# Dense layer, Mish, dense layer on one core: the first block of tokens in 128-token tiles, part of it transposed by DMA

## The chip, the core and the metric

The kernel runs on one core of a Trainium2 chip. The core has five engines with instruction streams of their own: TensorE (PE in the profile; PEld are its weight loads), VectorE (DVE), ScalarE (ACT), GpSimd (POOL) and SyncE (SP), which here only issues transfers. Transfers issued by SP and by ACT run on 16 DMA engines. The metric is device time in microseconds (us), the median of several runs.

## The reference

```python
h = jnp.einsum("bsd,df->bsf", x, w1) + b1
sp = jnp.log1p(jnp.exp(-jnp.abs(h))) + jnp.where(h > 0, h, jnp.zeros_like(h))
act = h * jnp.tanh(sp)
return jnp.einsum("bsf,fd->bsd", act, w2)
```

x is (1, 2048, 512), w1 (512, 1792), b1 (1792), w2 (1792, 512), all bf16. So there are 2048 tokens; h is x w1 + b1, act is Mish of h, and the output is act w2.

## The kernel before, in words

**Tiling.** Tokens go in four blocks of 512 (`NSB`), each of four tiles of 128. The first product wants x with its 512 features on the partitions, so x must be transposed: xT has four slices k of 128 features (`KT` = 4). The 1792 hidden features are 14 tiles f (`FT`). One tile of the first product, `mm1(t)`, is four matmuls (k = 0 to 3) of 128 rows by 512 tokens into one PSUM bank; ScalarE then computes Mish with b1 as bias from that bank into a_sb (`mish`, L167). One tile of the second product, `mm2(i)`, is 14 matmuls (one for each f) of 128 tokens by 512 outputs into a bank; VectorE casts it to bf16 (L202) and SP stores it (L180). The last tile, and only that one, is done in two parts so that its first part can be cast and stored while the second is computed.

**Order.** TensorE's order is written out by hand (L207 to L224): the first block's special start, then `mm1` for f = 4 to 13, then for each block its four `mm2` and the next block's 14 `mm1`. PSUM has eight banks. Tile t of the first product uses bank 4 + t mod 4 (`bank1`, L161), so a tile waits for the Mish of the tile four before it; the second product uses banks 0 to 3.

**Waits.** A `Stream` is one engine's queue. `mark` makes an instruction count up the engine's semaphore and returns a token, `wait` makes a queue wait for a token, `load` issues a transfer and returns its token. An engine's waits and instructions are executed in the order of the program; what stands behind a wait on its queue waits too. This is so for SP and ACT when they issue transfers.

**Loads (L88 to L102).** SP issues, in this order: the two halves (256 tokens each) of the first block of x, untransposed, into x_nat; w1 for f = 4 to 7; w1 for f = 8 to 13; w2; and the other three blocks of x by transposing DMAs straight into xT. ACT issues w1 for f = 0 to 3, in two pieces of two k slices, and b1. No wait stands between these.

**The start of the first block.** TensorE first runs six matmuls on a constant tile (`dummy`, L117) whose results nobody reads. Then `half_T(0)` (L122) transposes tokens 0 to 255 on TensorE, eight transposes of 128x128 against the identity; the results go from PSUM to xT by VectorE for even k and ScalarE for odd k, 256 columns at a time. Two more dummies of 256 columns follow. `first_mm1(h, ks)` (L140) then runs the first product for f = 0 to 3 and one half of the tokens, 256 columns a matmul: half 0 with k = 0, 1; then `half_T(1)`; half 0 with k = 2, 3; the transpose of b1 (L213), which arrives as 14 rows and is wanted as 14 columns; then half 1 with all k. Both halves of a tile share a bank and each starts a group of its own (`start=(k == 0)`).

The first block's tokens are dealt to the partitions so that a partition holds two neighbouring tokens (`x0v`), and its outputs are stored through the same view (`o0v`).

The change and the prediction's steps touch the loads, `half_T`, `first_mm1`, the dummies, `bank1`, `mm2`'s last tile, and the order at the end.

Of the kernel before, what the change touches and what calls it, by code (L numbers as in the profile page):

```python
# [4 lines left out]

P = 128
N_WARM = 6
FILL = (256, 256)


class Stream:
# [20 lines left out]
def bass_standalone__dense_activation_mish__prompt_kernel(  # L32
# [8 lines left out]
    ACT = mybir.ActivationFunctionType  # L41
    ALU = mybir.AluOpType
    BF, F32 = dt.bfloat16, dt.float32

    _, S, D = x.shape
    F = w1.shape[1]
    KT, FT, SBW = D // P, F // P, 512
    NSB, JT, H = S // SBW, SBW // P, D // 2
    assert (S, D, F) == (2048, 512, 1792)
    x2, out2 = x[0], out[0]  # L50
    w1v = w1.rearrange("(k p) f -> p k f", p=P)
    w2v = w2.rearrange("(j p) d -> p j d", p=P)
    F0 = 4

    with ExitStack() as es:
        def sb(name, shape, t):
            return es.enter_context(nc.sbuf_tensor(name, shape, t))

        x_nat = sb("x_nat", [P, JT, D], BF)
        xT = sb("xT", [P, KT, S], BF)  # L60
        w1_sb = sb("w1_sb", [P, KT, F], BF)
        w2_sb = sb("w2_sb", [P, FT, D], BF)
        b1_nat = sb("b1_nat", [FT, P], BF)
        b1_sb = sb("b1_sb", [P, FT], F32)
        ones = sb("ones", [P, P], BF)
        ident = sb("ident", [P, P], BF)
        a_sb = sb("a_sb", [P, NSB * FT, SBW], BF)
        o_sb = sb("o_sb", [P, NSB * JT, D], BF)
        ps = es.enter_context(nc.psum_tensor("ps", [P, 8, 512], F32))

        def sem(name):
            return es.enter_context(nc.semaphore(name))

        sp = Stream(nc.sync, None)
        pe = Stream(nc.tensor, sem("c_pe"))
        dve = Stream(nc.vector, sem("c_dve"))
        act = Stream(nc.scalar, sem("c_act"))
        pool = Stream(nc.gpsimd, sem("c_pool"))

        def load(q, dst, src, name, transpose=False):  # L80
            s = sem(name)
            (q.eng.dma_start_transpose if transpose else q.eng.dma_start)(dst, src).then_inc(s, 16)
            return (s, 16)

        n_pre = len(nc.cur_bb.bb.instructions)


        x0v = x2[0:SBW, :].rearrange("(h p j) d -> p h j d", h=2, j=2)  # L88
        t_xn = [load(sp, x_nat[:, 2 * h:2 * h + 2, :], x0v[:, h], "s_xn%d" % h) for h in range(2)]
        t_w1k = []  # L90
        for k in (0, 2):
            t_w1k += [load(act, w1_sb[:, k:k + 2, 0:F0 * P], w1v[:, k:k + 2, 0:F0 * P], "s_w1k%d" % k)] * 2
        t_b1 = load(act, b1_nat[:, :], b1.rearrange("(j p) -> j p", p=P), "s_b1")
        t_w1 = {}
        for a, b in ((4, 8), (8, FT)):
            t = load(sp, w1_sb[:, :, a * P:b * P], w1v[:, :, a * P:b * P], "s_w1_%d" % a)
            for f in range(a, b):
                t_w1[f] = t
        t_w2 = load(sp, w2_sb[:, :, :], w2v, "s_w2")
        t_xT = [None]  # L100
        for s in range(1, NSB):
            t_xT.append(load(sp, xT[:, :, s * SBW:(s + 1) * SBW], x2[s * SBW:(s + 1) * SBW, :], "s_xT%d" % s, True))  # L102

# [3 lines left out]
        t_id = pool.mark(pool.eng.affine_select(ident[:, :], ones[:, :], pattern=[[1, P]], compare_op=ALU.is_equal,  # L107
                                                fill=0.0, base=0, channel_multiplier=-1))
        act.eng.preload_act_table(ACT.Mish)  # L109


        warm = sb("warm", [P, 512], BF)
        pe.wait(dve.mark(nc.vector.memset(warm[:, :], 1.0)))  # L113
        c_w, c_m = warm[:, 0:P], warm

        def dummy(n=512):
            nc.tensor.matmul(ps[:, 7, 0:n], c_w, c_m[:, 0:n], start=True, stop=True)  # L117

        HB = SBW // 2
        t_cp = [[None] * KT for _ in range(2)]  # L120

        def half_T(h):  # L122

            pe.wait(t_xn[h])
            for k in range(KT):
                if h == 1:
                    pe.wait(t_cp[0][k])
                psb = ps[:, k, 0:HB // 2].bitcast(BF)
                for j in range(2):
                    mm = nc.tensor.transpose(psb[:, j * P:(j + 1) * P], x_nat[:, 2 * h + j, k * P:(k + 1) * P], ident[:, :])  # L130
                t = pe.mark(mm)
                dst = xT[:, k, h * HB:(h + 1) * HB]
                if k % 2 == 0:
                    dve.wait(t)
                    t_cp[h][k] = dve.mark(nc.vector.tensor_copy(dst, psb))  # L135
                else:
                    act.wait(t)
                    t_cp[h][k] = act.mark(act.eng.activation(dst, psb, ACT.Copy))  # L138

        def first_mm1(h, ks):  # L140

            cs = slice(h * HB, (h + 1) * HB)
            for k in ks:
                for f in range(F0):
                    pe.wait(t_w1k[k], t_cp[h][k])
                    mm = nc.tensor.matmul(ps[:, 4 + f, cs], w1_sb[:, k, f * P:(f + 1) * P], xT[:, k, cs],  # L146
                                          start=(k == 0), stop=(k == KT - 1))
                    if h == 1 and k == KT - 1:
                        mish(f, pe.mark(mm))

        for _ in range(N_WARM):
            dummy()
        pe.wait(t_id)
        half_T(0)
        for n in FILL:
            dummy(n)


        t_mish = {}

        def bank1(t):  # L161
            return 4 + t % 4

        def mish(t, t_mm):
            act.wait(t_b1c, t_mm)
            f = t % FT
            t_mish[t] = act.mark(act.eng.activation(a_sb[:, t, :], ps[:, bank1(t), :], ACT.Mish, bias=b1_sb[:, f:f + 1]))  # L167

        def mm1(t):
            s, f = divmod(t, FT)  # L170
            pe.wait(t_mish.get(t - 4), t_w1.get(f), t_xT[s])
            for k in range(KT):
                mm = nc.tensor.matmul(ps[:, bank1(t), :], w1_sb[:, k, f * P:(f + 1) * P],  # L173
                                      xT[:, k, s * SBW:(s + 1) * SBW], start=(k == 0), stop=(k == KT - 1))
            mish(t, pe.mark(mm))

        def store(q, i, lo, hi, tok):
            q.wait(tok)
            rows = out2[i * P:(i + 1) * P, :] if i >= JT else o0v[:, i // 2, i % 2, :]
            q.eng.dma_start(rows[:, lo:hi], o_sb[:, i, lo:hi]).then_inc(s_out, 16)  # L180

        s_out = sem("s_out")
        o0v = out2[0:SBW, :].rearrange("(h p j) d -> p h j d", h=2, j=2)
        n_out = 0
        t_ev = {}

        def mm2(i):
            nonlocal n_out
            s, j = divmod(i, JT)
            pe.wait(t_w2)  # L190
            last = i == NSB * JT - 1
            parts = [(0, H, i % 4), (H, D, (i + 1) % 4)] if last else [(0, D, i % 4)]
            for lo, hi, bank in parts:
                pe.wait(*([t_ev[bank]] if bank in t_ev else [t_b1c, t_cp[1][1], t_cp[1][3]]))
                for f in range(FT):
                    t = s * FT + f
                    pe.wait(t_mish[t])
                    mm = nc.tensor.matmul(ps[:, bank, 0:hi - lo], a_sb[:, t, j * P:(j + 1) * P], w2_sb[:, f, lo:hi],  # L198
                                          start=(f == 0), stop=(f == FT - 1))
                t_mm = pe.mark(mm)  # L200
                dve.wait(t_mm)
                t_ev[bank] = dve.mark(nc.vector.tensor_copy(o_sb[:, i, lo:hi], ps[:, bank, 0:hi - lo]))  # L202
                store(sp, i, lo, hi, t_ev[bank])
                n_out += 1


        first_mm1(0, (0, 1))  # L207
        half_T(1)
        first_mm1(0, (2, 3))
        pe.wait(t_b1)  # L210
        psb1 = ps[:, 0, 256:256 + FT // 2].bitcast(BF)
        pe.wait(t_cp[1][0])
        t_b1t = pe.mark(nc.tensor.transpose(psb1, b1_nat[:, :], ident[0:FT, 0:FT]))  # L213
        dve.wait(t_b1t)
        t_b1c = dve.mark(nc.vector.tensor_copy(b1_sb[:, :], psb1))  # L215
        first_mm1(1, range(KT))
        for t in range(F0, FT):
            mm1(t)
        for s in range(NSB):
            for j in range(JT):  # L220
                mm2(s * JT + j)
            if s + 1 < NSB:
                for f in range(FT):
                    mm1((s + 1) * FT + f)  # L224
# [37 lines left out]
```

## Time and profile before

| what | us |
|---|---|
| median of 11 runs | 106.59 |
| lowest and highest | 106.06, 107.3 |
| the profiled execution | 107.13 |
| its span, from first to last instruction | 105.9 |
| busy: TensorE, ScalarE, VectorE | 101.9, 40.6, 13.0 |
| last x half landed, after its issue | 4.1 |
| first, last L146 matmul start | 4.61, 9.57 |
| first L173 matmul starts | 10.59 |
| last CAST starts | 103.85 |

Busy times are sums over one execution's span; TensorE's include matmuls whose ends are modelled and overlap, so starts of matmuls are a better guide than their durations. The time around the span, 107.13 - 105.9 = 1.2 us, belongs to the execution and not to any engine. A line such as L146 is a line of the kernel as printed above. In the chain of work that ended last, each piece is what its successor waited for, or what stood before it on its engine.

### The profile page before, as it was taken

Reading aid. Unit: us, or ns where it says so; the run is one execution under the profiler, and the core shown is the slowest. Engines: PE = TensorE matmul, PEld = TensorE weight load, DVE = VectorE, ACT = ScalarE, POOL = GpSimd, SP = SyncE. Lnnn points to the kernel's source line nnn. Section 1 sums busy time; section 2 is a strip of 40 time slices with the busy share of each in tenths; the row PEclk is TensorE's granted clock in tenths of the full one; section 3 lists DMA queues with packets and bytes.
Section 4 is the critical chain, followed back from the end, with each engine's and each line's share of the span. In section 5 each row is a group of like instructions: output and inputs, shape, how many; then the busy total and the mean of one; then the engine's idle time right before and its main releaser. Section 6 shows DMA issues by size and latency. Waiting matters only on the chain.

```text
span 105.9 us, 1127 instructions
## 1 busy us (share of the span) xinstructions
PE 101.9 (96%) x494; PEld 49.5 (47%) x503; DVE 13.0 (12%) x23; ACT 40.6 (38%) x61; POOL 0.6 (1%) x6
## 2 busy tenths in 40 slices
PE   7997999999999999999999999999999999999992
PEld 2675444444444444444444444444444444444481
DVE  1210000022210000022112000021122000011241
ACT  3423988400007887500005888600005777700000
POOL 2000000000000000000000000000000000000000
DMA  5999999911111000001111000001111000001111
GB/s 138 372 373 352 346 246 219 99 42 48 50 50 50 0 0 6 0 0 50 50 50 50 0 0 3 0 6 50 50 50 50 0 0 0 0 0 56 50 50 50
DMA packets 12417, 7.94 MB, mean 75 GB/s; under 512 B 6652, under 2 KB 12156, under 8 KB 12412
## 3 DMA queue, kind: packets, MB, share of 16 engines
q1 hardware_dynamic: 11840, 7.34, 26.4%
q10 hardware_dynamic: 572, 0.53, 1.6%
q8 instruction: 4, 0.07, 0.3%
q14 instruction: 1, 0.01, 0.0%
HBM read 4.20 MB, written 2.10 MB: 59 GB/s over the span
## 4 chain that ended last, share of the span: by engine, by line
PE 96%; issue 1%; DVE 1%; ACT 1%; ACTq 0%
PE ps L198 46%; PE ps L173 42%; PE ps L146 4%; PE ps L117 3%; PE ps L130 1%; ACT a_sb L167 1%; DVE warm L113 0%; DVE o_sb L202 0%; PE ps L213 0%; ACTq L24 0%
## 5 line engine op out<-in xcount | busy, mean ns | idle before, releaser
L167 ACT ACTIVATE a_sb<-ps,b_sb 128x512 bf16<-128x512 f32 x56 | 37.9, 688 | 47.0 <-PE ps L173 44.9
L198 PE MATMUL ps<-w_sb,a_sb 128*128 128x512 bf16 (+1 forms) x234 | 48.8, 366 | 0.2
L173 PE MATMUL ps<-xT,w_sb 128*128 128x512 bf16 x203 | 45.1, 379 | 1.0 <-ACT a_sb L167 0.7
L198 PEld LDWEIGHTS ps<-w_sb,a_sb 128*128 128x128 bf16 x238 | 23.3, 98 | 25.3
L173 PEld LDWEIGHTS ps<-xT,w_sb 128*128 128x128 bf16 x208 | 20.3, 98 | 25.1 <-ACT a_sb L167 0.8
L202 DVE CAST o_sb<-ps 128x512 bf16<-128x512 f32 (+1 forms) x17 | 11.2, 660 | 84.8 <-PE ps L198 84.8
L146 PE MATMUL ps<-xT,w_sb 128*128 128x256 bf16 x32 | 4.9, 310 | 0.0
L117 PE MATMUL ps<-warm 128*128 128x512 bf16 (+1 forms) x8 | 3.4, 577 | 0.8 <-DVE warm L113 0.8
L146 PEld LDWEIGHTS ps<-xT,w_sb 128*128 128x128 bf16 x32 | 3.4, 111 | 0.7
L138 ACT ACTIVATE xT<-ps 128x256 bf16<-128x256 bf16 x4 | 1.4, 382 | 2.9 <-PE ps L130 2.9
L109 ACT ACT_TABLE_LOAD x1 | 1.3, 1283 | 1.8 <-issue 1.8
L130 PEld LDWEIGHTS ps<-ident,x_nat 128*128 128x128 bf16 x16 | 1.6, 130 | 0.7 <-issue 0.6
L117 PEld LDWEIGHTS ps<-warm 128*128 128x128 bf16 x8 | 1.0, 140 | 1.9 <-issue 1.1
L135 DVE COPY xT<-ps 128x256 bf16<-128x256 bf16 x4 | 1.1, 292 | 5.4 <-PE ps L130 5.3
L130 PE MATMUL ps<-ident,x_nat 128*128 128x128 bf16 x16 | 1.8, 274 | 0.0
L113 DVE MEMSET warm<- 128x512 bf16 x1 | 0.5, 485 | 0.2 <-issue 0.2
L107 POOL TENSOR_SCALAR_AFFINE_SELECT ident<-ones 128x128 bf16<-128x128 bf16 x1 | 0.3, 293 | 0.1
L215 DVE CAST b_sb<-ps 128x14 f32<-128x14 bf16 x1 | 0.2, 173 | 0.8 <-PE ps L213 0.8
L105 POOL MEMSET ones<- 128x128 bf16 x1 | 0.2, 204 | 0.0
L213 PEld LDWEIGHTS ps<-ident,b_nat 14*128 14x128 bf16 x1 | 0.1, 91 | 0.2 <-issue 0.2
L213 PE MATMUL ps<-ident,b_nat 14*128 14x14 bf16 x1 | 0.2, 178 | 0.0
L247 POOL MEMSET const-bfloat16-1.0<- 128x1 bf16 x1 | 0.1, 101 | 0.0
(3 smaller groups left out, 0.3 us busy)
## 6 DMA issues: line engine op xcount, KB each, us to landing
out_dram<-o_sb SPq DMA_DIRECT2D x15, 128.0 KB, 1.7
w_sb<-in_w_dram SPq DMA_DIRECT2D x1, 1792.0 KB, 12.1
w_sb<-in_w_dram SPq DMA_DIRECT2D x1, 768.0 KB, 7.5
x_nat<-in_x_dram SPq DMA_DIRECT2D x2, 256.0 KB, 3.5
w_sb<-in_w_dram ACTq DMA_DIRECT2D x2, 256.0 KB, 4.2
w_sb<-in_w_dram SPq DMA_DIRECT2D x1, 512.0 KB, 5.9
out_dram<-o_sb SPq DMA_DIRECT2D x2, 64.0 KB, 1.5
xT<-in_x_dram SPq DMA_TRANSPOSE x3, 6.1
```

Of the source, the lines that this page charges most:

```text
L109: act.eng.preload_act_table(ACT.Mish)
L113: pe.wait(dve.mark(nc.vector.memset(warm[:, :], 1.0)))
L117: nc.tensor.matmul(ps[:, 7, 0:n], c_w, c_m[:, 0:n], start=True, stop=True)
L130: mm = nc.tensor.transpose(psb[:, j * P:(j + 1) * P], x_nat[:, 2 * h + j, k * P:(k + 1) * P], ident[:, :])
L135: t_cp[h][k] = dve.mark(nc.vector.tensor_copy(dst, psb))
L138: t_cp[h][k] = act.mark(act.eng.activation(dst, psb, ACT.Copy))
L146: mm = nc.tensor.matmul(ps[:, 4 + f, cs], w1_sb[:, k, f * P:(f + 1) * P], xT[:, k, cs], start=(k == 0), stop=(k == KT - 1))
L167: t_mish[t] = act.mark(act.eng.activation(a_sb[:, t, :], ps[:, bank1(t), :], ACT.Mish, bias=b1_sb[:, f:f + 1]))
L173: mm = nc.tensor.matmul(ps[:, bank1(t), :], w1_sb[:, k, f * P:(f + 1) * P], xT[:, k, s * SBW:(s + 1) * SBW], start=(k == 0), stop=(k == KT ...
L198: mm = nc.tensor.matmul(ps[:, bank, 0:hi - lo], a_sb[:, t, j * P:(j + 1) * P], w2_sb[:, f, lo:hi], start=(f == 0), stop=(f == FT - 1))
L202: t_ev[bank] = dve.mark(nc.vector.tensor_copy(o_sb[:, i, lo:hi], ps[:, bank, 0:hi - lo]))
L213: t_b1t = pe.mark(nc.tensor.transpose(psb1, b1_nat[:, :], ident[0:FT, 0:FT]))
```

## The change

The first block goes by tiles of 128 tokens, and its second half comes transposed by DMA.

- Loads: SP issues x tile 0, x tile 1 (128 tokens each, plain rows, so `x0v` and `o0v` go), b1 (after VectorE has zeroed b1_nat, which is now 128x128), then waits for the last of w1's first pieces (`t_w1k[2]`), then issues the transposing DMA of tokens 256 to 511 into xT, w1 for f = 8 to 13, w2, and the other three transposing DMAs. ACT issues w1 for f = 0 to 3 in three pieces (k = 0, k = 1, k = 2 and 3) and w1 for f = 4 to 7 in two.
- The memset of the dummies' operand is 128 columns wide and stands first on VectorE; the dummies are 16 of 128 columns, and 2 after the first transposes.
- `part_T(j)` transposes one tile of 128 tokens, four transposes; all copies to xT are VectorE's.
- `first_mm1(js, fks)` runs any tiles js and pairs (f, k). The order: tile 0 with k = 0; transposes of tile 1; tile 0 with k = 1; tile 1 with k = 0, 1; both with k = 2; b1's transpose; both with k = 3; then f = 4 to 7 for both tiles, k outermost; then tiles 2 and 3 together for f = 0 to 7, f outermost.
- Banks: in the first block f = 4 to 7 use banks 0 to 3, all others stay at 4 + t mod 4. One table `t_bank` holds what each bank waits for. Each bank has one group: one start (tile 0, k = 0), one stop (tiles 2-3, k = 3).
- The last output tile is parted at column 384 instead of 256.

```diff
-N_WARM = 6
-FILL = (256, 256)
+N_WARM = 16
+N_FILL = 2
...
-        x_nat = sb("x_nat", [P, JT, D], BF)
+        x_nat = sb("x_nat", [P, 2, D], BF)
...
-        x0v = x2[0:SBW, :].rearrange("(h p j) d -> p h j d", h=2, j=2)
-        t_xn = [load(sp, x_nat[:, 2 * h:2 * h + 2, :], x0v[:, h], "s_xn%d" % h) for h in range(2)]
-        t_w1k = []
+        warm = sb("warm", [P, P], BF)
+        t_warm = dve.mark(nc.vector.memset(warm[:, :], 1.0))
+        t_b1z = dve.mark(nc.vector.memset(b1_nat[:, :], 0.0))
+        t_xa = load(sp, x_nat[:, 0, :], x2[0:P, :], "s_xa")
+        t_w1k = [load(act, w1_sb[:, k, 0:F0 * P], w1v[:, k, 0:F0 * P], "s_w1k%d" % k) for k in range(2)]
+        t_xb = load(sp, x_nat[:, 1, :], x2[P:2 * P, :], "s_xb")
+        t_w1k += [load(act, w1_sb[:, 2:4, 0:F0 * P], w1v[:, 2:4, 0:F0 * P], "s_w1k2")] * 2
+        sp.wait(t_b1z)
+        t_b1 = load(sp, b1_nat[0:FT, :], b1.rearrange("(j p) -> j p", p=P), "s_b1")
+        t_w1, t_w1m = {}, []
         for k in (0, 2):
-            t_w1k += [load(act, w1_sb[:, k:k + 2, 0:F0 * P], w1v[:, k:k + 2, 0:F0 * P], "s_w1k%d" % k)] * 2
-        t_b1 = load(act, b1_nat[:, :], b1.rearrange("(j p) -> j p", p=P), "s_b1")
-        t_w1 = {}
-        for a, b in ((4, 8), (8, FT)):
-            t = load(sp, w1_sb[:, :, a * P:b * P], w1v[:, :, a * P:b * P], "s_w1_%d" % a)
-            for f in range(a, b):
-                t_w1[f] = t
+            t_w1m += [load(act, w1_sb[:, k:k + 2, F0 * P:2 * F0 * P], w1v[:, k:k + 2, F0 * P:2 * F0 * P], "s_w1m%d" % k)] * 2
+        sp.wait(t_w1k[2])
+        t_xT = [load(sp, xT[:, :, 2 * P:SBW], x2[2 * P:SBW, :], "s_xT0", True)]
+        t = load(sp, w1_sb[:, :, 2 * F0 * P:F], w1v[:, :, 2 * F0 * P:F], "s_w1_8")
+        for f in range(2 * F0, FT):
+            t_w1[f] = t
         t_w2 = load(sp, w2_sb[:, :, :], w2v, "s_w2")
...
+        def part_T(j, tok):
+            pe.wait(tok)
             for k in range(KT):
+                pe.wait(t_cp.get((j - 1, k)))
+                psk = ps[:, k, 0:P // 2].bitcast(BF)
+                dve.wait(pe.mark(nc.tensor.transpose(psk, x_nat[:, j, k * P:(k + 1) * P], ident[:, :])))
+                t_cp[j, k] = dve.mark(nc.vector.tensor_copy(xT[:, k, j * P:(j + 1) * P], psk))
+
+        def first_mm1(js, fks):
+            cs = slice(js[0] * P, (js[-1] + 1) * P)
+            for f, k in fks:
+                pe.wait((t_w1k if f < F0 else t_w1m)[k])
+                if js[0] == 0 and k == 0:
+                    pe.wait(t_bank.get(bank1(f)))
+                pe.wait(*([t_cp[j, k] for j in js] if js[0] < 2 else t_xT))
+                mm = nc.tensor.matmul(ps[:, bank1(f), cs], w1_sb[:, k, f * P:(f + 1) * P], xT[:, k, cs],
+                                      start=(js[0] == 0 and k == 0), stop=(js[-1] == JT - 1 and k == KT - 1))
+                if js[-1] == JT - 1 and k == KT - 1:
+                    mish(f, pe.mark(mm))
...
         def bank1(t):
-            return 4 + t % 4
+            return t - F0 if F0 <= t < 2 * F0 else 4 + t % 4
...
         def mm1(t):
             s, f = divmod(t, FT)
-            pe.wait(t_mish.get(t - 4), t_w1.get(f), t_xT[s])
+            pe.wait(t_bank.get(bank1(t)), t_w1.get(f), t_xT[s])
...
-            parts = [(0, H, i % 4), (H, D, (i + 1) % 4)] if last else [(0, D, i % 4)]
+            parts = [(0, LC, i % 4), (LC, D, (i + 1) % 4)] if last else [(0, D, i % 4)]
...
-        first_mm1(0, (0, 1))
-        half_T(1)
-        first_mm1(0, (2, 3))
-        pe.wait(t_b1)
...
-        first_mm1(1, range(KT))
-        for t in range(F0, FT):
+        first_mm1([0], by_k(0, 0))
+        part_T(1, t_xb)
+        first_mm1([0], by_k(0, 1))
+        first_mm1([1], by_k(0, 0, 1))
+        first_mm1([0, 1], by_k(0, 2))
+        pe.wait(t_b1, t_cp[1, 3])
+        psb1 = ps[:, 3, 0:P // 2].bitcast(BF)
+        dve.wait(pe.mark(nc.tensor.transpose(psb1, b1_nat[:, :], ident[:, :])))
+        t_b1c = dve.mark(nc.vector.tensor_copy(b1_sb[:, :], psb1[:, 0:FT]))
+        t_bank[3] = t_b1c
+        first_mm1([0, 1], by_k(0, 3))
+        for k in range(KT - 1):
+            t_bank[k] = t_cp[1, k]
+        first_mm1([0, 1], by_k(F0, *range(KT)))
+        first_mm1([2, 3], [(f, k) for f in range(2 * F0) for k in range(KT)])
+        for t in range(2 * F0, FT):
             mm1(t)
```

In the changed kernel the matmuls of `first_mm1` stand on L145, those of `mm1` on L174, the transposes on L133 and their copies on L134; L167, L198, L202 and L180 stay what they are.

## The prediction

> **What bounds the kernel now.** I read the page's busy shares first, then the chain of work that ended last, then the waits, then a table of 2 us windows and the groups by shape.
>
> ```profile
> span 105.9 us, 1127 instructions
> PE 101.9 (96%) x494; PEld 49.5 (47%) x503; DVE 13.0 (12%) x23; ACT 40.6 (38%) x61; POOL 0.6 (1%) x6
> ```
>
> TensorE is busy 96% of the span. That alone doesn't say where time can be won, so the chain in order of time comes next:
>
> ```profile
> 0.79 2.74 PE ps L117 x6
> 3.53 0.85 PE ps L130 x8
> 4.39 0.43 PE ps L117 x2
> 4.81 1.71 PE ps L146 x8
> 6.52 0.49 PE ps L130 x8
> 7.01 0.87 PE ps L146 x8
> 7.88 0.11 PE ps L213
> 7.99 1.54 PE ps L146 x13
> ...
> 9.62 0.70 ACT a_sb L167
> 10.31 0.27 issue
> 10.59 8.58 PE ps L173 x39
> ...
> 103.85 0.42 DVE o_sb L202
> ```
>
> From 10.59 on the chain is TensorE nearly without a break: 432 matmuls of 512 columns' worth at a pitch of 0.2158 us (start to start in the trace) are 93.2 us, and 10.59 + 93.2 = 103.8, where the last CAST begins. So the only time to be had is ahead of 10.59 and behind 103.8. Ahead of it, the eight first L146 matmuls (256 columns) take 1.71 us and the next eight 0.87: the array runs at half pace until about 6.4 us. Behind L146 there is a hole:
>
> ```profile
> ACT a_sb L167 <- PE ps L146: 2.1, 1, 2.1
> PE ps L173 <- ACT a_sb L167: 0.7, 1, 0.7
> ```
>
> All four L146 tiles end within 0.33 us, at 9.7; the fifth tile needs the first one's bank, so TensorE stands until Mish 0 has run. The last L146 starts at 9.57, its successor at 10.59: 0.91 us beyond its own pitch of 0.109. Useful work between 4.61 (first L146) and 10.59 is 16 units of 0.2158, 3.45 us; the other 2.53 are the slow clock (0.83), eight transposes (0.53), the b1 transpose (0.2), the hole (0.91) and crumbs.
>
> The table of windows (us of the stretch; busy us and count of PE, weight loads, DVE, ACT, POOL; clock, DMA share, GB/s) shows that the loads run at their full rate from 4 us on, and less before:
>
> ```profile
> 2.00:4.00 2.00, 2.00 (x11) 1.08 (x10) 0.22 (x1) 1.11 (x2) 0.00 (x0) 1.00 1.00 326
> 4.00:6.00 2.00, 2.00 (x13) 1.50 (x12) 0.37 (x2) 0.76 (x2) 0.00 (x0) 1.00 1.07 374
> ```
>
> Two groups that the change resizes (mean ns behind the bar), and the transposing DMAs under the tile xT (ns of issue, least, middle and most):
>
> ```profile
> L135 DVE COPY xT<-ps 128x256 bf16<-128x256 bf16 x4 | 1.1, 292 | 5.4 <-PE ps L130 5.3
> L202 DVE CAST o_sb<-ps 128x256 bf16<-128x256 f32 x2 | 0.8, 425 | 1.9 <-PE ps L198 1.9
> ```
>
> ```profile
> L82 SPq DMA_TRANSPOSE xT<-in_x_dram x3: 2045/2443/11130, 2.7 to 16.0; - x3
> DMA to landing us min/median/max: 4.7/6.1/13.4
> ```
>
> **What the Trainium skill says.** "TensorE: Matmul & The Clock Gate", Part 1: the array runs at half clock until it has been busy through one free-running window of about 3.4 us. The trace agrees with the halves (427 against 216 ns per 512 columns); busy from 0.79, it turned at 6.42, as if a window from 3.0 to 6.4 had counted. A phase that varies by run would also fit the spread of the times, 106.06 to 107.3. "DMA: Bandwidth & Descriptors", Queues, rings and completion order: each DMA engine goes round-robin over the queues it has work for, a packet of descriptors at a time. The packet records agree: x half 0 (1.0 to 2.4), w1 (2.0 to 3.4), x half 1 (2.8 to 4.0), w1 (3.5 to 4.7), so SP's and ACT's loads alternate. The same page, Latency and other measured facts, gives a DMA transpose 261 GB/s; here two of 512 KB back to back took 4.43 us (13.01 to 17.44), 237 GB/s. "PSUM — Partial Sum Buffer", The four PSUM rules: a group's first matmul clears the marks of its whole bank and later ones overwrite where no mark stands, which is why one start per bank is enough; no time hangs on it.
>
> **The change, step by step**, in the clock phase of this profile.
>
> (1) Loads. Before w1's second piece 1024 KB had to come, landing at 5.26. Now up to w1k2 it is 768 KB. Reading the old packets' running sum, 768 KB had started by 3.8 us; with the 0.56 us that the old piece took from last packet to landing, about 4.35. x tile 0 is half the old first load: packets 1.02 to about 1.8 instead of 2.41, landing about 2.25 (was 2.85). w1k0 then about 2.8, x tile 1 3.2, w1k1 3.6, w1m0 and w1m2 4.9 and 5.6. b1 moves to SP behind x tile 1 and its zeroing memset is done long before.
>
> (2) Start. The memset of 128 columns lets PE start at about 0.5; 16 dummies at 0.107 end at 2.2. Four transposes start at 2.4 (landing plus wait and weight load). The first result is there 0.31 later; a 128-column DVE copy, from 0.292 for 256 and 0.16 fixed (both CAST rows: 0.692 at 512, 0.425 at 256), is 0.225; so tile 0's first slice is usable at about 3.1, and the other four transposes and two dummies fill until 3.04. First real matmul 3.1 instead of 4.61: -1.5 us.
>
> (3) From there TensorE has work and data, at half pace: k=0 of tile 0 (4 x 0.107) to 3.5, transposes of tile 1 (0.43) to 3.96, then 12 matmuls of 128 columns (1.28) to 5.24, k=2 (4 x 0.213) to 6.1, b1 to 6.2, one matmul of k=3 until the clock turns at 6.42, three at 0.109 to 6.75, and 16 for tiles 4 to 7 to 8.50. Copies run on DVE alone (0.225 each, four per tile), ahead of their users by 0.2 us or more.
>
> (4) x tiles 2-3. SP waits for w1k2, so until 4.35; behind that wait on SP stand this transpose, the rest of w1, w2 and the other three transposes. From issue to first packet: 1.0 us (the first x load: issue 0.0, packets 1.02) to at most 1.45 (third transpose: issue 15.99, packets 17.44). 256 KB at 237 GB/s: 1.1. Last packet to landing: 0.5 to 1.2 (the three transposes). Landing 6.95 to 8.1, needed at 8.50: hidden, at no cost; without that cover each late us costs one.
>
> (5) 32 matmuls of 256 columns at 0.1092: 3.49, to 11.99 with eight f tiles done. The kernel before has done them at 10.59 + 16 x 0.2158 = 14.04. So -2.05. As a sum: start -1.5, hole -0.91, slow clock +0.52 (1.35 instead of 0.83), transposes -0.1 (0.43 for 0.53), b1 -0.1, narrower matmuls +0.05. The hole goes because eight banks instead of four hold tiles: the ninth tile (at 11.99) wants bank 4, Mish 0 of which starts at 9.1 and ends at 9.8. ACT falls behind (a tile each 0.44, Mish 0.57 back to back), is through eight at 13.7, and the next reuse is at 15.45.
>
> (6) Later loads. Rest of w1: behind the transpose, 768 KB at the 0.37 MB per us of the windows, lands about 9.6, needed at 11.99. w2: lands about 14.9 (was 14.07), needed at 11.99 + 24 x 0.2158 = 17.2. The other transposes come a us later and are needed from 29 us. All hidden, with 2.3 us to spare.
>
> (7) Tail. 384 + 128 columns instead of 256 + 256: the matmuls are the same columns (14 x 0.162 + 14 x 0.056, the transposes' warm pitch), the last CAST falls from 0.425 to about 0.29: -0.13. The last store is half as big; between -0.1 and +0.1 for its shorter rows, taken as nothing.
>
> Sum -2.2. Against the profiled execution (107.13 us, span 105.9): 104.95. That execution was 0.54 above the median, so I subtract from the median: 104.4; with 0.1 for a wait or two of semaphores that I left out, **104.5 us**.
>
> **Rivals.** (A) The clock turns a window later. The new start leaves small gaps (2.2 to 2.4, perhaps up to 3.1), and a window that holds one may not count. For: a window that was busy about 65% (-0.4 to 3.0) did not count in this trace. Against: the gaps are under a tenth of a window and from 3.1 there are none. It would cost half of 3.4, 1.7 us: 106.2. (B) Slow first loads: small transfers have more fixed cost. If x tile 0 landed at 2.85 and x tile 1 at 4.0, as their bytes would in the old order, +0.6: 105.1. It can't be much more: the k=2 matmuls start at 5.24 in my count, and the old kernel, with 256 KB more ahead of it, had this weight at 5.26. (C) Ends slower: the moved transpose lands late. If a DMA transpose takes its 6.1 us median to landing, 4.35 + 6.1 = 10.45, a stall of 1.95: 106.4, no change; from 10.7 on the kernel is slower than before, and at 12.5 it would be 108.4. For: the first transpose held SP for 11.13 us. Against: that was behind 3 MB of w1 and w2 on the same queue, and here the queue is empty. (D) The gain in the head is eaten by w2, which starts later: it would need w2 2.3 us later than worked out, little speaks for it.
>
> **How the numbers follow.** Sum as worked out, with B as its upper end: 0.72, own range 103.8 to 105.4. A: 0.12. C with under 2.2 us of stall: 0.07. C beyond, or D: 0.09. About 0.5% (0.53 us) is what these runs tell from no change. Faster takes the first, a good part of A and of early C: 0.82; same 0.09; slower 0.09. The range 103.8 to 106.1 leaves out the rest of A and C above it and the small chance of more gain below.
>
> **What would show it.** Right: first L145 at about 3.1; half pitch until about one window's end, no gap of TensorE from 3.1 to 12; the ninth tile (first L174) at about 12.0 with no wait on ACT; xT's first landing before 8.5. Wrong: L145 waiting on the transposing DMA before its 256-column second half, half pitch past 7.6, or L198 waiting for w2.

## The result and the profile after

The changed kernel takes 121.88 us (median of 12 runs, 121.35 to 123.3) against 106.67 for the kernel before (47 runs): a ratio of 1.1446, 95% interval 1.1411 to 1.1481. The forecast was 104.5 us, so the sign was wrong, and the loss of 15.2 us is larger than any rival allowed for as likely. The page of the changed kernel (busy shares, slices of the span, the group of the first block's matmuls):

```profile
span 121.2 us, 1184 instructions
PE 102.5 (85%) x520; PEld 51.8 (43%) x529; DVE 12.9 (11%) x28; ACT 39.3 (32%) x57; POOL 0.6 (1%) x6
...
PE   8960000199999999999999999999999999999993
...
PEclk9998555558999999999999999999999999999999
...
L145 PE MATMUL ps<-xT,w_sb 128*128 128x256 bf16 (+1 forms) x72 | 10.4, 314 | 15.9 <-DMA xT<-in_x_dram 15.6
```

TensorE's busy time is nearly the old one, 102.5 against 101.9 us: no work was added. Four slices of 3 us each are empty, and the last column of the group says what ended that: a transfer into xT, waited for 15.6 us. The clock row drops to half in the pause. The chain shows which transfer it was (start, length, what):

```profile
7.68 9.48 SPq L82
...
17.20 2.04 SPq L82
...
19.29 4.25 DMA xT<-in_x_dram
...
23.68 5.87 PE ps L145 x32
...
29.60 5.13 PE ps L174 x23
...
119.41 0.29 DVE o_sb L202
```

The transposing DMA of x tiles 2-3, the only one that the next matmuls need, was issued at 5.16 and landed at 8.39. The three issues in this chain, at 7.68, 17.20 and 19.29, are the transposing DMAs of the other three blocks; the last landed at 23.54, and 0.14 us later TensorE goes on. So the matmuls of tiles 2-3 waited for transposes that are wanted much later. The code says the same:

```python
pe.wait(*([t_cp[j, k] for j in js] if js[0] < 2 else t_xT))
```

`t_xT` is a list. When `first_mm1([2, 3], ...)` is called, all four tokens are in it, and the star hands all of them to `wait`. The prediction priced this line as a wait for the first.

Everything after fits: the ninth f tile has its first record at 29.60, where by its own first record the kernel before reached it at 14.04 (10.59 + 16 x 0.2158), 15.56 earlier; the last CAST starts at 119.41 instead of 103.85, again 15.56 later. The whole loss lies ahead of 29.60.

Both of these starts are one matmul too late, since each trace lacks its first record. The chains count 39 matmuls for the last ten f tiles of the first block in the kernel before, and 23 for the last six here; 40 and 24 were issued. From first record to last CAST the kernel before takes 93.26 us, and the eight-banks kernel below, whose records are complete, 93.48 for the same 432 matmuls: one pitch more. The true starts are then 10.37 and 29.39. So the hole in the kernel before, read as 0.91 us in the prediction, was 0.69, and that kernel reached its ninth f tile at 13.82.

### The profile page after: what moved, and what is told of

It is laid out like the page before. It is cut to its first block, busy times and chain, and to the rows that moved or that the text cites. A ratio compares the mean times of both kernels' runs of the same rounds, so it can differ in the third digit from the quotient of the medians.

```text
span 121.2 us, 1184 instructions
## 1 busy us (share of the span) xinstructions
PE 102.5 (85%) x520; PEld 51.8 (43%) x529; DVE 12.9 (11%) x28; ACT 39.3 (32%) x57; POOL 0.6 (1%) x6
## 4 chain that ended last, share of the span: by engine, by line
PE 79%; SPq 11%; DMA 7%; issue 1%; ACTq 1%; DVE 0%
PE ps L198 40%; PE ps L174 34%; SPq L82 11%; PE ps L145 5%; DMA xT<-in_x_dram 4%; DMA w_sb<-in_w_dram 3%; ACTq L82 1%; DVE o_sb L202 0%
## 5 line engine op out<-in xcount | busy, mean ns | idle before, releaser
L167 ACT ACTIVATE a_sb<-ps,b_sb 128x512 bf16<-128x512 f32 x56 | 38.1, 687 | 66.1 <-PE ps L174 44.5
L198 PE MATMUL ps<-w_sb,a_sb 128*128 128x512 bf16 (+2 forms) x233 | 48.8, 366 | 0.3
L174 PE MATMUL ps<-xT,w_sb 128*128 128x512 bf16 x188 | 41.7, 379 | 0.2
L198 PEld LDWEIGHTS ps<-w_sb,a_sb 128*128 128x128 bf16 x238 | 22.8, 98 | 25.9
L174 PEld LDWEIGHTS ps<-xT,w_sb 128*128 128x128 bf16 x192 | 18.8, 98 | 22.5
L145 PE MATMUL ps<-xT,w_sb 128*128 128x256 bf16 (+1 forms) x72 | 10.4, 314 | 15.9 <-DMA xT<-in_x_dram 15.6
L202 DVE CAST o_sb<-ps 128x512 bf16<-128x512 f32 (+2 forms) x17 | 11.2, 660 | 102.4 <-PE ps L198 102.4
L145 PEld LDWEIGHTS ps<-xT,w_sb 128*128 128x128 bf16 x72 | 7.6, 118 | 18.2 <-issue 15.9
L123 PE MATMUL ps<-warm 128*128 128x128 bf16 x18 | 2.3, 313 | 0.4 <-DVE warm L88 0.4
L123 PEld LDWEIGHTS ps<-warm 128*128 128x128 bf16 x18 | 1.9, 148 | 0.4 <-DVE warm L88 0.4
L134 DVE COPY xT<-ps 128x128 bf16<-128x128 bf16 x8 | 1.2, 216 | 2.8 <-PE ps L133 2.8
L133 PE MATMUL ps<-ident,x_nat 128*128 128x128 bf16 x8 | 1.2, 308 | 0.1
L133 PEld LDWEIGHTS ps<-ident,x_nat 128*128 128x128 bf16 x8 | 0.8, 140 | 0.4 <-issue 0.4
```

The lines of the kernel that those rows point to most:

```text
L123: nc.tensor.matmul(ps[:, 7, 0:P], warm[:, :], warm[:, :], start=True, stop=True)
L133: dve.wait(pe.mark(nc.tensor.transpose(psk, x_nat[:, j, k * P:(k + 1) * P], ident[:, :])))
L134: t_cp[j, k] = dve.mark(nc.vector.tensor_copy(xT[:, k, j * P:(j + 1) * P], psk))
L145: mm = nc.tensor.matmul(ps[:, bank1(f), cs], w1_sb[:, k, f * P:(f + 1) * P], xT[:, k, cs], start=(js[0] == 0 and k == 0), stop=(js[-1] == ...
L202: t_bank[bank] = dve.mark(nc.vector.tensor_copy(o_sb[:, i, lo:hi], ps[:, bank, 0:hi - lo]))
```

## Experiments

**One wait instead of four.**

```diff
-                pe.wait(*([t_cp[j, k] for j in js] if js[0] < 2 else t_xT))
+                pe.wait(*([t_cp[j, k] for j in js] if js[0] < 2 else t_xT[:1]))
```

> The changed kernel with one edit: the matmuls of x tiles 2-3 wait for the transposing DMA of those tiles alone (landed 8.39 us in the changed kernel's profile) and not for all four transposing DMAs (the last landed 23.54). Theory W (the wait list is the loss): TensorE stops only from 7.87 to about 8.5, the ninth f tile starts near 12.0, w2 (landed 17.46) is met at about 17.2 and costs up to 0.3 us; time 104.4 to 105.0. Theory T (a transposing DMA ahead of w1 and w2 makes the first block's data late whatever is waited for): the stop moves to the next load and the time stays above 115.

Measured: 106.56 us (22 runs, 105.61 to 106.93), beside 106.42 for the kernel before on the same chip; ratio 1.0004, interval 0.9982 to 1.0027. So the loss is gone and the list was its cause. But the gain that the prediction had worked out is not there: both theories missed. The chain of its profile has a load as its longest piece in the head:

```profile
6.75 10.76 DMA w_sb<-in_w_dram
17.51 0.05 issue
17.56 12.26 PE ps L198 x56
```

This is w2, issued at 6.75 and landed at 17.51. TensorE was through its first product at 16.74 and stood 0.82 us. The ninth f tile (L174) had started at 11.56, against 13.82 in the kernel before: 2.26 us were won in the head, and 0.82 of them given back at w2. This is the fastest execution (105.61 us); where the median loses about 1 us more isn't in this profile.

**The same wait in the kernel before.**

```diff
         first_mm1(1, range(KT))
+        pe.wait(*t_xT[1:])
         for t in range(F0, FT):
```

> The kernel before with one wait added: ahead of the fifth f tile TensorE waits for all three transposing DMAs (the last landed 22.10 us). Theory W: that wait alone reproduces the loss. TensorE stands from 9.7 to 22.2 instead of to 10.59, +11.6, and comes back at half pace for one window, +1.7 to +2.3: 120 to 121 us. Theory T: the kernel before has the same data early, so a wait for loads it does not need yet costs little, under 110 us.

Measured: 120.08 us (4 runs), ratio 1.1253, interval 1.1191 to 1.1315. The timeline of TensorE has the pause in brackets, with what ended it:

```profile
21.16 11.13 PE L173 MATMUL ps<-xT,w_sb 128*128 128x512 bf16 x40 [11.82 <-DMA xT<-in_x_dram]
32.12 1.24 PE L198 MATMUL ps<-w_sb,a_sb 128*128 128x512 bf16 x5
```

One wait for loads that come in good time for their real use, put at the wrong place, reproduces the loss in a kernel that has nothing else of the change. From the first of the 40 matmuls to the first of the second product (L198) it is 10.96 us, where 40 x 0.2158 = 8.63 are needed: the pause also costs 2.3 us of clock.

**Busy while it waits.** In the changed kernel, with its four-fold wait, ahead of `first_mm1([2, 3], ...)`:

```diff
+        pe.wait(t_zer)
+        for _ in range(140):
+            nc.tensor.matmul(ps[:, 7, 2 * P:SBW], warm[:, :], zer[:, :], start=False, stop=False)
```

> The changed kernel, with the four-fold wait kept, and 140 matmuls of a zero operand (256 columns, added into the still empty half of one bank) run ahead of it, so that TensorE is busy while it waits. Theory W with a clock loss on top: the stop stays, but the 21 matmuls that ran at 0.213 us after it run at 0.109, so 2.2 us less than the changed kernel: 119.7. If the clock costs nothing of its own: 121.9.

Measured: 121.81 us (4 runs), as the changed kernel. Judged by the time alone, the slow clock would cost nothing of its own; the profile says otherwise. TensorE's timeline (L225 are the added matmuls, L147 is the old L145):

```profile
8.47 15.45 PE L225 MATMUL ps<-zer,warm 128*128 128x256 bf16 x140
25.72 3.65 PE L147 MATMUL ps<-xT,w_sb 128*128 128x256 bf16 x32 [1.80 <-DMA xT<-in_x_dram]
```

The clock is kept: 3.65 us for 32 matmuls instead of 5.87, so of the loss 2.2 us is slow clock after the pause. The time didn't fall because the last transpose landed at 25.58 instead of 23.54 here. That the loads were later because TensorE was busy isn't shown; a possible cause, for up to half of it, stands in the last section.

**Eight banks alone, in the kernel before.**

```diff
         def bank1(t):
-            return 4 + t % 4
+            return t - F0 if F0 <= t < 2 * F0 else 4 + t % 4
...
-            pe.wait(t_mish.get(t - 4), t_w1.get(f), t_xT[s])
+            pe.wait(t_ev.get(bank1(t)), t_w1.get(f), t_xT[s])
```

with `t_ev` also holding the Mish of each bank, and for banks 0 to 3 at first the copies out of them.

> The kernel before with one part of the change: f tiles 4 to 7 of the first block use banks 0 to 3, so that eight tiles are held and the fifth does not wait for the first Mish. By the prediction's step 5 the hole of 0.91 us goes: about 105.7. If the hole only moves to a later wait (on ACT, or on the load of w1 for f = 8 to 13, landed 8.89), no change: 106.6.

Measured: 105.98 us (22 runs), ratio 0.9934, interval 0.9909 to 0.9959, which on 106.42 is 0.4 to 1.0 us. The chain now runs from L146 into the next f tiles with nothing between:

```profile
8.13 1.85 PE ps L146 x16
9.98 8.63 PE ps L174 x40
```

A chain counts a matmul from the end of the one before it; the timeline has the first L174 start at 9.82, one pitch of 0.11 after the last L146 (9.71):

```profile
9.82 1.46 PE L174 MATMUL ps<-xT,w_sb 128*128 128x512 bf16 x6
```

Step 5's term for the hole holds, with the 0.69 us that it really had; 0.91 is at the upper end of what was measured.

**Four ways to have w2 earlier.** All start from the one-wait kernel. Without SP's wait:

```diff
-        sp.wait(t_w1k[2])
```

> The one-wait kernel without SP's wait for w1k2 ahead of the transposing DMA of x tiles 2-3. The one-wait kernel is left with TensorE standing 0.82 us for w2 (landed 17.51 us in its profile). Theory D (late loads: SP issues nothing until w1k2 has landed at 4.75, the DMA engines are half empty from 6 to 9, so w2 is 3 us late and sets the end): w2 lands at about 14.5 and the stop at w2 goes, but w1k2 and w1m share the engines with the transposing DMA and come 0.7 to 2 us later: 105.3 to 106.5. Theory C (the clock: in most runs the array turns to full pace later than in the profile, and loads are not the limit): w2 early, time unchanged at 106.5.

Measured: 107.27 us (18 runs), ratio 1.0055, interval 1.0026 to 1.0084. Neither theory: w2 didn't come early (18.32), and the first weights came late. Waits of TensorE (us in total, times, longest; L144 is the old L145):

```profile
PE ps L144 <- DMA w_sb<-in_w_dram: 3.1, 3, 1.5
```

w1k2 landed at 6.33 instead of 4.75, the last piece of w1 for f = 4 to 7 at 10.15 instead of 6.22, and the transpose itself, though issued at 1.42, at 10.34 instead of 7.90. So SP's wait isn't mere delay: without it the transpose, w1 and w2 run beside the loads wanted first, and those lose.

A shorter wait:

```diff
-        sp.wait(t_w1k[2])
+        sp.wait(t_w1k[1])
```

> The one-wait kernel with SP waiting for w1k1 (landed 3.44 us) instead of w1k2 (4.75) ahead of the transposing DMA. Theory D: everything SP issues after it comes 1.3 us earlier, w2 at about 16.2, ahead of its use; the time falls by the stop at w2, 0.8 to 1.5 us: 105.0 to 105.7. Theory C: no change, 106.5.

Measured: 104.98 us (6 runs, 104.81 to 105.16), ratio 0.9845, interval 0.981 to 0.9881. The chain has no load after 5.7:

```profile
6.41 5.68 PE ps L145 x52
12.09 5.18 PE ps L174 x24
17.27 12.09 PE ps L198 x56
```

w2 landed at 16.96, just ahead of its first use at 17.1. What is left is the stop for w1k2, here 1.1 us (4.6 to 5.74).

w2 in two pieces of seven f tiles, each with its own wait:

```diff
-        t_w2 = load(sp, w2_sb[:, :, :], w2v, "s_w2")
+        t_w2 = [load(sp, w2_sb[:, a:a + 7, :], w2v[:, a:a + 7, :], "s_w2_%d" % a) for a in (0, 7)]
...
-            pe.wait(t_w2)
...
-                    pe.wait(t_mish[t])
+                    pe.wait(t_w2[f // 7], t_mish[t])
```

> The one-wait kernel with w2 loaded in two pieces of seven f tiles, each with its own wait. Loads start no earlier, but the first piece lands about 2.5 us before the second, and the second is wanted 1.5 us after the first. Theory D: the stop at w2 shrinks by up to 1.5 us: 105.1 to 105.7. Theory C: 106.5.

Measured: 105.68 us (6 runs), ratio 0.9895, interval 0.9847 to 0.9943. The pieces landed at 15.53 and 17.98; no stop at w2 is left. In this profile TensorE stood 0.5 us for w1 for f = 8 to 13 instead (landed 12.43), and its ninth f tile starts only at 12.57.

> Both: SP waits for w1k1, and w2 in two pieces. Theory D: no stop is left after the first block's start, and the prediction's sum (2.2 us under the kernel before) applies: 104.4 to 104.9. Theory C: 106.5.

Both edits together: 105.12 us (6 runs), ratio 0.9848, interval 0.9806 to 0.989. No better than the shorter wait alone: once w2 isn't waited for, splitting it has nothing to win. The last three runs all go the way of theory D, and none shows the clock theory's unchanged 106.5. D's ranges held for the first two; this one stayed 0.2 above its own.

**The tail.** The shorter-wait kernel with `LC = 256` instead of 384.

> The kernel with SP's wait on w1k1 (104.98 us, its runs within 0.35 us of each other), with the last output tile parted at 256 as in the kernel before. By the prediction's step 7 the parting at 384 saves 0.13 us in the last CAST and nothing in the last store: 105.1. If the shorter rows of the last store (256 bytes) cost what the CAST saves: 105.0 or less.

Measured: 105.47 us (6 runs), ratio 0.9896, interval 0.9853 to 0.994. That overlaps the interval at 384 (0.981 to 0.9881), so the time doesn't decide. The chains end

```profile
101.94 0.29 DVE o_sb L202
```

for 384 and

```profile
101.69 0.42 DVE o_sb L202
```

for 256, both with a span of 103.7 (103.74 and 103.72): 1.80 us from the start of the last CAST to the end against 2.03. The CAST is 0.13 shorter as forecast, and the smaller store gives about another 0.1.

**w1k2 in two pieces.** In the shorter-wait kernel:

```diff
-        t_w1k += [load(act, w1_sb[:, 2:4, 0:F0 * P], w1v[:, 2:4, 0:F0 * P], "s_w1k2")] * 2
+        t_w1k += [load(act, w1_sb[:, k, 0:F0 * P], w1v[:, k, 0:F0 * P], "s_w1k%d" % k) for k in (2, 3)]
```

> The kernel with SP's wait on w1k1, and w1k2 loaded as two pieces (k = 2, k = 3) instead of one. In its profile TensorE stood 1.1 us for w1k2, whose engines finished between 3.88 and 5.70 us. If the piece for k = 2 lands half its share earlier, the stop shrinks by about 0.5 us: 104.5. If one slow DMA engine sets the landing whatever the size, no change: 105.0.

Measured: 105.18 us (6 runs, 104.67 to 106.29), ratio 0.9854, interval 0.9811 to 0.9897: no gain to be seen. The pieces did come earlier, at 4.75 and 5.41 us where the whole had landed at 5.70, so it isn't so that one slow DMA engine sets the landing whatever the size. TensorE waited for neither of them (the row of the timeline holds the last twelve matmuls of 128 columns and the first four of k = 2, which have 256, with no idle time between):

```profile
4.11 2.27 PE L145 MATMUL ps<-xT,w_sb 128*128 128x128 bf16 x16
```

But in this execution the array ran at half pace until 6.2 us, against 4.0 in the profile of the shorter-wait kernel, and TensorE was ready for k = 2 only at 5.39, against 4.64 there. Half pace took the place of the stop: with a missing first record allowed for, the ninth f tile starts at 11.95, and there at 11.92. An execution of the split kernel that turns to full pace early isn't on record. Why the DMA engines finished w1k2 so unevenly in the shorter-wait kernel (3.88 to 5.70) stays open.

**The one-wait kernel again.**

> The one-wait kernel once more, for its profile: the first profile was its fastest execution (105.61 us against a median of 106.56), with w2 landing at 17.51. Theory D: an execution near the median has w2 landing about 1 us later, 18.5, and the second product starting right there. Theory C: w2 lands near 17.5 and the array turns to full pace later.

Measured: one execution of 106.04 us, 0.43 more than the first profile's. Its chain:

```profile
7.12 10.83 DMA w_sb<-in_w_dram
...
17.99 12.26 PE ps L198 x56
```

w2 landed at 17.95, and the second product starts at 17.99 instead of 17.56: 0.43 later, the whole difference between the two executions. SP had issued behind its wait at 5.14 instead of 4.77, since w1k2 landed that much later. The landing of w2 sets this kernel's end in both. Both are faster than the median of 106.56, so theory D's 18.5 for an execution near it wasn't put to the test.

## Why the prediction was wrong, point by point

**Step 4 failed, on the wait and not on the transfer.** It asked when the transpose of tiles 2-3 lands and when it is needed (8.39 measured, 6.95 to 8.1 forecast; it would have been needed at 7.87, at a cost of half a microsecond; the one-wait kernel's two profiles show 0.47 and 0.55, where the prediction had none). It didn't ask what the instruction waits for. The wait names four transfers, the last of which landed at 23.54. The loss in terms of this profile: without any stop the 32 matmuls would have run from 7.87 to 11.36; the pause is 15.81 (7.87 to 23.68), and the slow clock 2.2: 29.4, where the ninth tile starts. The one-wait kernel and the kernel before with the wait added show it from both sides. Rival C had the sign and the place, a transposing DMA that the first block waits for, but the wrong transfer: it priced the moved one, and the 9 in 100 for a slower kernel weighed only that and a late w2.

**Step 6 failed second, and the first failure hid it.** w2 was to land at 14.9 with 2.3 us to spare. It landed at 17.46, and in the one-wait kernel at 17.51, where it stopped TensorE for 0.82 us. In the changed kernel the whole error was made ahead of w2: the rest of w1 landed at 12.20 instead of 9.6, and w2 followed in 5.26 us (5.3 forecast). In the one-wait kernel it was 11.42, and 6.09 us for w2. Windows of the changed kernel and of the kernel before (us; busy us of PE, weight loads, DVE, ACT, POOL; clock, DMA share, GB/s):

```profile
6.00:8.00 2.00, 2.00 (x19) 1.49 (x17) 0.06 (x1) 0.00 (x0) 0.00 (x0) 1.00 0.81 153
8.00:10.00 2.00, 0.04 (x1) 0.00 (x0) 0.00 (x0) 0.00 (x0) 0.00 (x0) 1.00 0.80 225
```

```profile
6.00:8.00 2.00, 2.00 (x21) 1.58 (x20) 0.52 (x2) 0.66 (x2) 0.00 (x0) 1.00 1.06 371
8.00:10.00 2.00, 1.84 (x16) 1.41 (x16) 0.17 (x1) 0.38 (x1) 0.00 (x0) 1.00 1.10 352
```

In these 4 us the kernel before moved 1.45 MB, the changed one 0.76: 0.69 MB, 1.9 us of loads at 0.36 MB per us. The step let the loads follow each other without a gap. In fact SP woke at 5.16 (forecast 4.35), the transpose's packets ran from 6.5 to 7.7, and behind them the packets of w1 came up to their full rate only at about 9. w2's distance to its use was the term to doubt: the prediction dismissed its rival D with "little speaks for it", and D is what the kernel met once the list was mended.

**Steps 1 to 3 were right up to w1k1; the loads behind it were late.** x tile 0 landed at 2.26 (forecast 2.25), w1k0 at 2.59 (2.8), x tile 1 at 2.95 (3.2), w1k1 at 3.31 (3.6); but w1k2 at 5.14 (4.35), its engines done between 3.96 and 5.14, and the two pieces for f = 4 to 7 at 6.06 and 6.71 (4.9 and 5.6). The first real matmul started at 3.07 (3.1), a copy took 0.214 (0.225). TensorE reached tiles 2-3 at 7.87 (8.50), since the array turned to full pace at about 4.3 in this execution instead of 6.4; a stop of 0.4 us for w1k2 came of it. The notes of the Trainium skill, "TensorE: Matmul & The Clock Gate", Part 1, say that where the window falls varies from run to run; the profiles of the new head fit that, with the turn between about 3.9 us (one-wait) and 6.5 (both edits). Rival A (the clock a window later) wasn't seen in any profile of the new head. Rival B (slow first loads) doesn't hold for the x tiles; w1k2 and the two pieces behind it were 0.8 to 1.2 us late.

**Step 5** gave the right sum, in part by luck: the ninth f tile starts at 11.56 and 12.07 in the one-wait kernel's two profiles, and at 11.92 with the shorter wait, against 11.99 forecast. In the first of them three stops that the sum didn't have (w1k2 0.34, the transpose 0.47, the rest of w1 0.11) came to 0.9 us, and an array that turned at 3.9 us instead of 6.4 made up for them: 10 matmuls at 0.107 instead of 0.056 are about 0.5 us of slow clock (1.35 forecast). The hole was 0.69 and not 0.91. **Step 7** is right: 0.13 for the CAST, and about 0.1 for the store that was taken as nothing.

With the list mended and SP's wait shortened the change gains most of what was forecast of it: 104.98 us beside 106.69 for the kernel before, 1.7 us of the forecast 2.2, ratio 0.9845. That version is faster than both kernels. Of the parts of the change only the eight banks and the tail were tried alone; the earlier start is read from profiles.

## What to carry over

Before pricing a transfer, write down for every wait which tokens it holds at the moment the instruction is issued: a list that is still growing, or grown full, can name loads that nobody needs yet, and then the last of them sets the time. When work is moved forward, recompute the slack of the next load against the new, earlier use, and let no transfer start in the sum before its queue can issue it. A queue's wait can be worth its delay where it keeps bulk loads away from the ones wanted first: here neither the longest wait (106.56) nor none (107.27) was best, but one in between (104.98).

## What was not expected of the hardware

A pause of TensorE of 15.8 us put the array back to half pace for 4.6 us (23.68 to 28.3) in the changed kernel, and one of 12 us for 4.8 us (21.16 to 25.9) in the kernel before with the wait added. A zero operand was enough to keep full pace (32 matmuls in 3.65 us instead of 5.87).

The time from the landing of w1 for f = 8 to 13 to that of w2 behind it (1792 KB) falls in two groups. In four profiles (5.19, 5.26, 5.24 and 5.22 us: the kernel before, the changed kernel, the all-waits and the eight-banks kernels) no instruction fetch happened in between. In the seven others with w2 in one piece it was 5.43 to 6.57 us (5.43, 5.81, 6.01, 6.05, 6.09, 6.21, 6.57), and in each of them a fetch of 16 KB, 1.1 to 1.2 us long on a DMA queue of its own, began in that stretch. The fetch moves with how far TensorE has come: it began at 12.8 us in the one-wait kernel, at 19.0 in the kernel before, and at 25.0 in the changed kernel, just after its pause. TensorE at work doesn't explain the two groups: it was busy in the kernel before and the eight-banks kernel (5.19 and 5.22) as in the one-wait kernel (6.09). That the fetch holds up one DMA engine, and w2 with it, fits these numbers; no run was made to show it.
